# Retention by 64 tokens of two batches at a time, with every small matmul on a quarter of the array

## The chip, the cores and the metric

The kernel runs on one core of a Trainium2 chip. Its time is the device time of one execution in microseconds (us). All operands are fp32. The profile calls TensorE's matmuls PE and its weight loads PEld; DVE is VectorE, ACT is ScalarE, POOL is GpSimd, and SP is the engine that issues most of the DMAs. TensorE's array has 128 rows (the contracted index) and 128 columns (the partitions of the result). A matmul that contracts over 64 and gives 64 partitions covers a quarter of it, one with 128 and 64 covers half. In the records one fp32 matmul is two MATMUL records, each with a weight load.

## The reference

A retention layer gives 3072 tokens of 512 features, and a two-layer network with the activation h * sigmoid(1.702 h) follows.

```python
# q, k, v: (batch 4, heads 8, tokens 768, dim 64), fp32
gamma = 1 - 2 ** (-5 - arange(8))
state = 0
for t in range(768):
    state = gamma * state + outer(k[:, :, t], v[:, :, t])     # 64 x 64 per batch and head
    y[:, :, t] = q[:, :, t] @ state / sqrt(64)
x = y as (3072 tokens, 512)
h = x @ w_in                                                  # 512 x 2048
out = (h / (1 + exp(-1.702 * h))) @ w_out                     # 2048 x 512
```

The weights come in as 64-bit numbers.

## The kernel before

**Blocks.** The 3072 tokens are worked on in six blocks of 512. Retention makes x of a block, `up0`, `up1` (blocks 0 and 1) or `up` (the others) multiply it by w_in, `hidden` applies the activation, and `down` multiplies by w_out. `up` and `down` use a scheme of seven products in place of eight (the `sums_*` functions form the operands), on full 128x128 weights.

**Chunks.** Retention goes by 24 chunks of 128 tokens of one batch, so a sequence has six chunks (`NC`). With c the place in the sequence, a chunk has these steps for its eight heads:

- `turn`: q and k are brought to (dim, token). For chunks 0 to 7 ("early") by TensorE transposes with the identity and two ACT copies (line 242); for the others ("late") by DVE transposes (line 245) of tiles that 32 small DMAs per chunk put in the right blocks (line 148).
- `scores` (line 269): k times q, contraction over the 64 dims, for 128 keys by 128 queries, in two halves of the keys: quarter-array matmuls with 128 moving columns. Late chunks leave out the queries ahead of the keys' half, so half of their scores matmuls have 64 columns.
- `decayed`: DVE multiplies the scores by the decay mask (line 295 early, lines 288, 291 and 292 late), giving `at`. Late chunks keep `at` in a layout of their own (`at2`, `moved`), with a second set of decay columns (`cold2`) and a rebuilt mask.
- `finish`: q times the old state (line 328, quarter array, not for c = 0); `at` times v added to it in the same PSUM (line 328, mostly half array: 128 keys contracted, 64 columns); k decayed (`kd`, a POOL multiply at line 260) times v (line 351, half array, not for the last c), for the state. DVE then scales the sum into X (line 355) and updates the state (line 358 or 361, after a POOL multiply at line 360).

`attend(j, f)` issues the scores of chunk j and the finish of chunk f.

**Weights.** `fetch` starts a 512 KB DMA of raw weights on SP's queue (line 175) into one of three buffers. `narrow` turns 64-bit weights into fp32 with one ACT step (line 204) and six DVE steps (lines 205 to 214), and fetches again. There are 2 narrow calls of half size and 15 of full size.

**Order.** TensorE runs in the order in which the program gives its instructions; for the other engines a planner chooses the order within the dependencies, except for instructions marked `keep_in_program_order`. The program issues chunk 0 to 4 with narrows and the first three `up0` units; then 13 `up0` units with chunks 5 to 7 between them; then 16 `up1` units; then `down(0)`, `down(1)`, and for blocks 2 to 5 `up` and `down`. The late chunks sit between units of `down`. At the start SP gets the loads of chunk 0 (q and v; k goes on ACT's queue), one weight fetch, the loads of chunk 1, and one more fetch. POOL's queue loads `cold` and `rowd`; the mask is built from `cold` by eight DVE copies (line 548) and one POOL select (line 551). `keep_warm` issues TensorE transposes whose results are not used.

Of the kernel before, what the change touches and what calls it, by code (L numbers as in the profile page):

```python
# [9 lines left out]
F32 = mybir.dt.float32  # L10
# [18 lines left out]
def kernel(  # L29
# [36 lines left out]
    NC = S // P  # L66
    NCH = B * NC
# [8 lines left out]
    assert 2 * D == P and HP * P == DM and S % P == 0 and NCH % CB == 0 and DM == 512 and NFF == 16  # L76
# [19 lines left out]
    rowd = const.tile([P, HP, P], F32, name="rowd")  # L96
    cold = const.tile([P, 2 * H], F32, name="cold")
    cold2 = const.tile([P, 2 * H], F32, name="cold2")
    at2 = const.tile([P, 2, HP, P], F32, name="at2")
    whole = const.tile([P, 2, 2], F32, name="whole")  # L100
    ident = const.tile([P, P], F32, name="ident")
    mask = const.tile([P, 2, HP, P], F32, name="mask")
    state = [const.tile([P, HP, D], F32, name=f"state{i}") for i in range(2)]
# [4 lines left out]
    def late(j):  # L108

        return j >= 2 * CB

    def moved(r, s):

        return r ^ s // 2

    def load(j, what="qkv"):


        b, c = divmod(j, NC)
        rows = slice(c * P, (c + 1) * P)

        def plain(name, src, tag, bufs, pairs=False, engine=sp):
            t = two.tile([P, H, D], F32, name=name + "_in", tag=tag, bufs=bufs)
            QKV[name, j] = t
            src = src[b, :, rows, :].rearrange("h p d -> p h d")
            if late(j):
                for i in range(2):
                    sp.dma_start(t[:, 6 * i:6 * i + 2, :], src[:, 6 * i:6 * i + 2, :])  # L130
                    sp.dma_start(t[i * D:(i + 1) * D, 2:6, :], src[(1 - i) * D:(2 - i) * D, 2:6, :])
            elif pairs:
                for i in range(2):
                    engine.dma_start(t[:, i:H:2, :], src[:, i * HP:(i + 1) * HP, :])
            else:
                sp.dma_start(t, src)

        if j < 2 * CB:
            if "q" in what:
                plain("q", q, "q_sq", 2, True)  # L140
                plain("kn", k, "k_sq", 2, True, sp if j else act)
        elif "q" in what:
            for name, src in (("q", q), ("k", k)):
                t = two.tile([P, HP, P // C4, C4], F32, name=name + "_sq")
                for r0 in range(0, P, C4):
                    d0 = r0 % D
                    for hp in range(HP):
                        tc.keep_in_program_order(sp.dma_start(
                            t[r0:r0 + C4, hp],
                            src[b, hp + HP * (r0 // D), rows, d0:d0 + C4].rearrange("(s p) d -> p s d", p=C4)))  # L150
                QKV[name, j] = t
        if "v" in what:
            if j >= 2 * CB and c < NC - 1:
                plain("kn", k, "kn", 1)
            plain("v", v, "v", 2)
# [62 lines left out]

    QT, KT, KD, AT = {}, {}, {}, {}

    def home(j, name):

        at = ["qT", "kT", "kd", "at"].index(name)
        shape = [[HP, P], [HP, P], [H, D], [2, HP, P]][at]
        if j >= 2 * CB:
            return at2 if at == 3 else one.tile([P] + shape, F32, name=name, tag=name, bufs=2 - (at > 0))
        if at < 3:
            t = G[:, at, j % 2 * 2:j % 2 * 2 + 2]
            return t.rearrange("p s t -> p (s t)").rearrange("p (a b) -> p a b", a=shape[0])
        return G[:, 3 + j % 2].rearrange("p s t -> p (s t)").rearrange("p (a b c) -> p a b c", a=2, b=HP)  # L230

    def turn(j, between=lambda: None):

        early = j < 2 * CB
        for name, store in (("q", QT), ("k", KT)):
            t = home(j, name + "T")
            if early:
                x = QKV["kn", j] if name == "k" else QKV.pop(("q", j))
                p = ps.tile([P, HP, P], F32, name="pt", tag="y")
                for hp in range(HP):  # L240
                    pe.transpose(p[:, hp, :], x[:, 2 * hp:2 * hp + 2, :].rearrange("p i d -> p (i d)"), ident)
                act.activation(t, p, AF.Copy)
                between()
            else:
                tc.keep_in_program_order(dve.transpose(
                    t.rearrange("p h t -> p (h t)"), QKV.pop((name, j)).rearrange("p h s d -> p (h s d)")))
            store[j] = t
        if early:
            decay(j)
        if j + 2 < NCH and (j + 2 < 2 * CB or not early):  # L250
            load(j + 2, "qk")

    def decay(j):

        if j % NC == NC - 1:
            return
        KD[j] = home(j, "kd")
        x = QKV.pop(("kn", j)).rearrange("p h d -> p (h d)")
        x = x.rearrange("p (s r d) -> p r s d", s=HP, r=2) if j < 2 * CB else x.rearrange("p (r s d) -> p r s d", r=2, s=HP)
        pool.tensor_mul(KD[j].rearrange("p (r s) d -> p r s d", r=2), x,  # L260
                        (cold2 if late(j) else cold)[:, H:2 * H].rearrange("p (r s) -> p r s", r=2)[:, :, :, None].to_broadcast([P, 2, HP, D]))

    def scores(j):
        p = ps_a.tile([P, 2, HP, P], F32, name="pa", tag="pa")
        kt, qt = KT.pop(j), QT[j]

        def product(r, s, h, t0):
            c, k = (h ^ moved(r, s) if late(j) else h) * D, slice(r * D, (r + 1) * D)
            pe.matmul(p[c:c + D, r, s, t0:], kt[k, s, h * D:(h + 1) * D], qt[k, s, t0:], start=True, stop=True)  # L269

        if late(j):

            for s in range(2):
                for r, o, h in ((0, 0, 0), (0, 0, 1), (1, 0, 1), (1, 0, 0), (0, 2, 0), (1, 2, 0), (0, 2, 1), (1, 2, 1)):
                    product(r, s + o, h, h * D)
        else:
            for s in range(HP):
                for h in range(2):
                    for r in range(2):
                        product(r, s, h, 0)  # L280
        return p

    def decayed(j, p):

        a = AT[j] = home(j, "at")
        if late(j):

            dve.tensor_mul(a[:, :, :, D:], p[:, :, :, D:], mask[:, :, :, D:])  # L288
            a, x, m = [t.rearrange("p r s t -> p (r s) t") for t in (a, p, mask)]
            a2, x2, m2 = [t[:D].rearrange("p (g e) t -> p g e t", g=4)[:, 0:4:3, :, :D] for t in (a, x, m)]  # L290
            dve.tensor_mul(a2, x2, m2)
            dve.tensor_mul(a[D:, 2:6, :D], x[D:, 2:6, :D], m[D:, 2:6, :D])
        else:
            for i in range(2):
                dve.tensor_mul(a[:, i], p[:, i], mask[:, i])  # L295

    def attend(j, f=None):


        p = []  # L300
        if f is not None:
            finish(f, lambda: j is not None and p.append(scores(j)))
        else:
            p.append(scores(j))
        if j is not None:
            decayed(j, p[0])
            if j > 2 * CB:
                decay(j)
        if f is not None and f + 2 < 2 * CB:
            load(f + 2, "v")  # L310
        if j is not None and 2 * CB < j < NCH - 1:
            load(j + 1, "v")

    def finish(j, between):
        c = j % NC
        old, new = state[c % 2], state[(c + 1) % 2]
        vn, a, qt = QKV.pop(("v", j)), AT.pop(j), QT.pop(j)


        y = ps_a.tile([P, 2, HP, P], F32, name="py", tag="py")  # L320
        heads = [(s, r) for s in range(HP) for r in range(2)]
        started = set()

        def add(r, s, v, x, t):

            first = (r, s % 2) not in started
            started.add((r, s % 2))
            pe.matmul(y[s % 2 * D:(s % 2 + 1) * D, r, s // 2, t], v, x, start=first, stop=False, skip_group_check=True)  # L328

        if not late(j):  # L330
            between()
        if c:
            for s, r in heads:
                k = slice(r * D, (r + 1) * D)
                add(r, s, old[k, s, :], qt[k, s, :], slice(0, P))
        if late(j):


            for s, r in heads[:HP]:
                k = slice(r * D, (r + 1) * D)  # L340
                add(r, s, vn[k, HP * r + s, :], a[k, r, s, :D], slice(0, D))
            between()
        for s, r in heads:
            t = slice(D if late(j) and s < 2 else 0, P)
            add(r, s, vn[:, HP * r + s, :], a[:, r, s, t], t)
        if c < NC - 1:

            kd = KD.pop(j)
            u = y[:, 0, 2:4, :].rearrange("p o t -> p (o t)").rearrange("p (s d) -> p s d", s=HP)
            for s, r in heads:  # L350
                pe.matmul(u[r * D:(r + 1) * D, s, :], kd[:, HP * r + s, :], vn[:, HP * r + s, :],  # L351
                          start=False, stop=True, skip_group_check=True)
        half, t0 = divmod(j % CB * P, TH)
        x = X1 if j // CB == 1 else X
# [325 lines left out]
```

## Time and profile before

| what | value |
|---|---|
| median of 16 runs | 699.07 us (698.22 to 700.41) |
| the profiled execution's own time | 699.25 us |
| its span in the profile | 697.5 us |
| PE, DVE, ACT, POOL busy | 98%, 52%, 18%, 20% of the span |
| bytes moved by DMA | 46.4 MB |

The span runs from the first to the last instruction of the profiled execution. A group of instructions is named by engine, line, and out<-in tiles; "mean" is the duration of one record, and as matmuls overlap, durations do not add up to time. The windows view gives busy time of each engine in a stretch, with the number of records in brackets. The chain of waits is followed back from the last instruction; its pieces are start, length and what ran.

### The profile page before, as it was taken

The numbers are of one execution on the slowest core, as the hardware profiler recorded it, in microseconds if no ns is written. First come the engines' busy times: TensorE is split into PE (matmuls) and PEld (weight loads), VectorE is DVE, ScalarE is ACT, GpSimd is POOL, SyncE is SP. The second block draws the span as 40 slices with busy tenths as digits, with TensorE's granted clock in tenths as the row PEclk, the third lists the DMA queues.
The fourth block names the chain that finished last, engine by engine and source line by source line (L and its number), as shares of the span: only waits on it lengthen the run. The fifth ranks groups of instructions, "written<-read, shape, count | busy, mean of one in ns | idle before, by whom it ended". The sixth has DMA issues, their size and how long they took to land.

```text
span 697.5 us, 11471 instructions
## 1 busy us (share of the span) xinstructions
PE 680.9 (98%) x4621; PEld 569.1 (82%) x4621; DVE 365.1 (52%) x541; ACT 125.8 (18%) x197; POOL 137.6 (20%) x137
## 2 busy tenths in 40 slices
PE   6699999999999999999999999999999999999997
PEld 5588885446888888888888888888888888888886
DVE  2998889994710843443652444463345372344241
ACT  2213333221000001332000332000333000233000
POOL 4211031000366414000324100134100143000030
PEclk9999999999999999999999999999999999999999
DMA  9995443522121223200323320323320210000001
GB/s 212 264 221 166 136 137 111 157 35 32 29 35 57 62 43 94 50 13 14 69 42 73 70 41 8 66 35 73 70 42 2 51 40 17 30 1 1 15 1 45
DMA packets 140404, 46.40 MB, mean 67 GB/s; under 512 B 131824, under 2 KB 132864, under 8 KB 140352
## 3 DMA queue, kind: packets, MB, share of 16 engines
q1 hardware_dynamic: 136096, 38.84, 24.8%
q0 software_dynamic: 2112, 5.53, 2.3%
q10 hardware_dynamic: 2144, 1.31, 0.6%
q8 instruction: 36, 0.59, 0.4%
q14 instruction: 16, 0.13, 0.1%
HBM read 39.34 MB, written 6.29 MB: 65 GB/s over the span
## 4 chain that ended last, share of the span: by engine, by line
PE 88%; DVE 7%; DMA 2%; SPq 1%; ACT 1%; issue 1%; POOL 1%; ACTq 0%; DVEq 0%; POOLq 0%
PE pd L491 39%; PE px L440 16%; PE py L440 12%; PE ph L401 8%; PE py L328 5%; PE ph L388 5%; PE pa L269 2%; PE py L351 1%; DMA kn_in<-in_k_dram 1%; DMA W<-in_moe_w_in_dram 1%; DVE W L430 1%; DVE G L430 1%; DVE W L214 1%; DVE W L210 1%; DVE G L295 1%
## 5 line engine op out<-in xcount | busy, mean ns | idle before, releaser
L491 PE MATMUL pd<-W,G 128*128 128x256 f32 x1120 | 247.4, 381 | 0.4 <-DVE G L431 0.3
L491 PEld LDWEIGHTS pd<-W,G 128*128 128x128 f32 x1120 | 211.3, 190 | 30.6 <-DVE G L431 1.2
L440 PE MATMUL px<-X,W 128*128 128x256 f32 x512 | 119.0, 379 | 0.0
L440 PEld LDWEIGHTS px<-X,W 128*128 128x128 f32 x512 | 97.3, 190 | 13.2
L440 PE MATMUL py<-X,W 128*128 128x256 f32 x384 | 90.7, 379 | 0.0
L440 PEld LDWEIGHTS py<-X,W 128*128 128x128 f32 x384 | 73.0, 190 | 9.9
L388 PE MATMUL ph<-X,W 128*128 128x256 f32 x256 | 58.0, 383 | 1.6 <-DVE W L214 0.9
L401 PE MATMUL ph<-W,W 128*128 128x512 f32 x128 | 55.2, 593 | 0.2 <-DVE W L355 0.2
L260 POOL TENSOR_TENSOR kd<-kn_in,cold 128x512 f32<-128x512 f32 x13 | 13.7, 1056 | 210.7 <-DMA k_sq<-in_k_dram 117.0
L388 PEld LDWEIGHTS ph<-X,W 128*128 128x128 f32 x256 | 47.8, 190 | 8.8 <-DVE W L214 1.3
L288 DVE TENSOR_TENSOR at<-pa,mask 128x512 f32<-128x512 f32 x16 | 11.0, 689 | 74.1 <-PE py L328 65.4
L401 PEld LDWEIGHTS ph<-W,W 128*128 128x128 f32 x128 | 24.2, 190 | 30.7 <-issue 28.5
L432 POOL TENSOR_TENSOR G<-G 128x512 f32<-128x512 f32 x20 | 29.5, 1481 | 95.0 <-DVE G L431 93.6
L369 DVE TENSOR_TENSOR G<-G,sg 128x512 f32<-128x512 f32 x48 | 33.0, 689 | 13.7 <-ACT sg L367 13.7
L367 ACT ACTIVATE sg<-G 128x512 f32<-128x512 f32 x48 | 30.2, 630 | 51.0 <-DVE G L450 30.7
L483 POOL DMA_DIRECT2D out_dram<-o x20 | 14.9, 748 | 119.9 <-DVE o L482 119.9
L367 ACT ACTIVATE sg<-ph 128x512 f32<-128x512 f32 x32 | 19.2, 600 | 100.1 <-PE ph L388 48.9
L491 PE MATMUL pd<-W,W 128*128 128x256 f32 x160 | 35.8, 381 | 0.4 <-DVE W L431 0.3
L491 PEld LDWEIGHTS pd<-W,W 128*128 128x128 f32 x160 | 30.2, 190 | 5.6 <-DVE W L431 1.2
L450 DVE TENSOR_TENSOR G<-py,p 128x512 f32<-128x512 f32 x16 | 11.1, 692 | 37.7 <-PE py L440 37.7
L478 ACT ACTIVATE u<-pd 128x512 f32<-128x512 f32 x6 | 3.6, 597 | 146.0 <-PE pd L491 146.0
L482 DVE TENSOR_TENSOR o<-pd,vv 128x512 f32<-128x512 f32 x12 | 7.7, 686 | 34.9 <-ACT vv L478 34.9
(106 smaller groups left out, 679.1 us busy)
## 6 DMA issues: line engine op xcount, KB each, us to landing
W<-in_moe_w_in_dram SPq DMA_DIRECT2D x12, 512.0 KB, 4.9
W<-in_moe_w_out_dram SPq DMA_DIRECT2D x10, 512.0 KB, 4.2
out_dram<-o POOLq DMA_DIRECT2D x20, 256.0 KB, 2.8
v_in<-in_v_dram SPq DMA_DIRECT2D x64, 64.0 KB, 2.4
q_sq<-in_q_dram SPq DMA_DIRECT2D x256, 16.0 KB, 1.8
k_sq<-in_k_dram SPq DMA_DIRECT2D x256, 16.0 KB, 1.8
kn_in<-in_k_dram SPq DMA_DIRECT2D x52, 64.0 KB, 2.4
G<-in_moe_w_out_dram SPq DMA_DIRECT2D x6, 512.0 KB, 3.9
```

What stands on the lines that cost most here:

```text
L260: pool.tensor_mul(KD[j].rearrange("p (r s) d -> p r s d", r=2), x, (cold2 if late(j) else cold)[:, H:2 * H].rearrange("p (r s) -> p r s", ...
L269: pe.matmul(p[c:c + D, r, s, t0:], kt[k, s, h * D:(h + 1) * D], qt[k, s, t0:], start=True, stop=True)
L328: pe.matmul(y[s % 2 * D:(s % 2 + 1) * D, r, s // 2, t], v, x, start=first, stop=False, skip_group_check=True)
L367: act.activation(s, h, AF.Sigmoid, scale=1.702)
L369: dve.tensor_mul(g, h[:, i], s[:, i])
L388: pe.matmul(h[:, ab], w, X[:, 2 * half + c // 2, c % 2, :], start=(ab == 0 and c == 0), stop=(c == 3), skip_group_check=True)
L401: pe.matmul(h, w, X1[:, c // 2:4:2, c % 2, :], start=(c == 0), stop=(c == 3))
L430: dve.tensor_sub(a[2], a[0], a[2])
L432: pool.tensor_sub(a[1], a[1], a[0])
L440: pe.matmul(acc[:, u, :], W1[:, 2 * d + u, sa, c, :], X[:, sb, c, :], start=(start and u == 0 and c == 0), stop=(stop and c == 1), skip_gr ...
L483: (pool if m < NB - 1 else act).dma_start(rows[th, e], o)
L491: pe.matmul(p0[:, n, :], g1(m, p, sa)[:, n * P:(n + 1) * P], W2[:, sb, p, :], start=(new and p == 0 and n == 0), stop=(last and p == NP - ...
```

## The change

A chunk is now 64 tokens of two batches: partitions 0 to 63 hold one batch, 64 to 127 the other. There are still 24 chunks, in two sequences of twelve (`NC = S // D`), and four of them still make a block of 512 tokens. Every small matmul has a contraction of 64, 64 columns and 64 moving columns, and is issued so that four in a row lie on the four quarters: the scores, k times v, q times the state, `at` times v, and the early turns, which are matmuls with the identity now and no transposes. q times the state is no longer added to `at` times v in PSUM: it has a region of its own, and DVE multiplies it by `rowd` and adds the rest. The update of the state lies in the second half of the `pa` tile and no longer in `py`. The special layouts of late chunks (`at2`, `moved`, `cold2`, the second mask) are gone.

At the start the first weight fetch goes ahead of v of chunk 0 and the second ahead of the loads of chunk 1, a narrow is called ahead of `turn(0)`, `rowd` and the mask come from one DMA, and the order of the first chunks changes.

```diff
-    NC = S // P
-    NCH = B * NC
+    NC = S // D
+    NCH = B // 2 * NC
...
-    state = [const.tile([P, HP, D], F32, name=f"state{i}") for i in range(2)]
+    state = [const.tile([P, 2, HP, D], F32, name=f"state{i}") for i in range(2)]
...
+            for i in range(2):
+                engine.dma_start(t[i * D:(i + 1) * D], src[b + i, :, rows, :].rearrange("h p d -> p h d"))
...
-                    for hp in range(HP):
+                    for n in range(P // C4):
+                        t0 = c * D + n * C4 % D
                         tc.keep_in_program_order(sp.dma_start(
-                            t[r0:r0 + C4, hp],
-                            src[b, hp + HP * (r0 // D), rows, d0:d0 + C4].rearrange("(s p) d -> p s d", p=C4)))
+                            t[r0:r0 + C4, :, n], src[b + n * C4 // D, h0:h0 + HP, t0:t0 + C4, d0:d0 + C4]
+                            .rearrange("h p d -> p h d")))
...
+    HALF = [slice(i * D, (i + 1) * D) for i in range(2)]
+    TWO = [(i, r) for i in range(2) for r in range(2)]
...
+            x = QKV.pop(("q", j)), QKV["kn", j]
+            p = [ps.tile([P, 2, HP, D], F32, name="pt", tag="y") for i in range(2)]
+            order = [(n, s, i, r) for n in range(2) for s in range(HP) for i, r in TWO]
+            for n, s, i, r in sorted(order, key=lambda o: o[2]) if j == 0 else order:
+                pe.matmul(p[i][HALF[r], n, s, :], x[n][HALF[i], HP * r + s, :], ident[HALF[i], HALF[i]],
+                          start=True, stop=True)
...
+            for i in range(2):
+                act.activation(t[:, :, :, HALF[i]], p[i], AF.Copy)
...
+    def attend(j, f=None):
+
+        pa = ps_a.tile([P, 2, 2, HP, D], F32, name="pa", tag="pa")
+        if j is not None:
             for s in range(HP):
+                for r, i in TWO:
+                    pe.matmul(pa[HALF[i], r, 0, s, :], KT[j][HALF[r], s, HALF[i]], QT[j][HALF[r], s, HALF[i]],
+                              start=True, stop=True)
+            KT.pop(j)
+        if f is not None:
+            c = f % NC
+            old, new = state[c % 2], state[(c + 1) % 2]
+            vn, a, qt = QKV.pop(("v", f)), AT.pop(f), QT.pop(f)
+            if c < NC - 1:
+                kd = KD.pop(f)
+                for s in range(HP):
+                    for i, r in TWO:
+                        pe.matmul(pa[HALF[r], i, 1, s, :], kd[HALF[i], HP * r + s, :], vn[HALF[i], HP * r + s, :],
+                                  start=True, stop=True)
+            py = ps_a.tile([P, 2, 2, 2, P], F32, name="py", tag="py")
+            if c:
+                for s2 in range(2):
+                    for i in range(2):
+                        for r, o in TWO:
+                            pe.matmul(py[HALF[o], r, 1, i, s2 * D:(s2 + 1) * D], old[HALF[r], i, 2 * s2 + o, :],
+                                      qt[HALF[r], 2 * s2 + o, HALF[i]], start=True, stop=True)
+            for s2 in range(2):
+                for r in range(2):
+                    for i, o in TWO:
+                        s = 2 * s2 + o
+                        pe.matmul(py[HALF[o], i, 0, r, s2 * D:(s2 + 1) * D], vn[HALF[i], HP * r + s, :],
+                                  a[HALF[i], r, s, :], start=True, stop=True)
+        if j is not None:
+            AT[j] = home(j, "at")
+            dve.tensor_mul(AT[j], pa[:, :, 0], mask)
             if j > 2 * CB:
                 decay(j)
+        if f is not None:
...
+            if c:
+                tmp = two.tile([P, 2, 2, P], F32, name="tmp", bufs=1)
+                dve.tensor_mul(tmp, py[:, :, 1].rearrange("p r i t -> p i r t"),
+                               rowd.rearrange("p (r s) t -> p r (s t)", r=2)[:, None].to_broadcast([P, 2, 2, P]))
+                dve.tensor_add(x, y, tmp.rearrange(by, t=D))
+            else:
+                act.activation(x, y, AF.Copy)
+            u = pa[:, :, 1]
+            if c == 0:
+                dve.tensor_copy(new, u)
+            elif c < NC - 1:
+                pool.tensor_mul(new, old, whole[:, None, :, None].to_broadcast([P, 2, HP, D]))
+                dve.tensor_add(new, new, u)
+            if f + 2 < 2 * CB:
+                load(f + 2, "v")
...
-    load(0)
+    load(0, "qk")
     make_identity(nc, ident)
...
+        pool.dma_start(cold[HALF[i]].rearrange("p (n h) -> p n h", n=2),
+                       bass.AP(tensor=col_decay.tensor, offset=col_decay.offset, ap=[[W, D], [D * W + H, 2], [1, H]]))
+    pool.dma_start(m3, bass.AP(tensor=row_decay.tensor, offset=row_decay.offset, ap=[[0, P], [P, H], [1, D]]))
...
     fetch()
+    load(0, "v")
+    fetch()
     load(1)
-    fetch()
...
+    for o in range(2):
+        act.activation(rowd[HALF[o]], m3[HALF[o], o:H:2, :], AF.Copy)
+
+    dve.tensor_mul(m3, m3, cold[:, 0:H, None].to_broadcast([P, H, D]))
+    for i in range(2):
+        pool.affine_select(out=m3[HALF[i]], in_=m3[HALF[i]], compare_op=ALU.is_ge, fill=0.0, base=0,
+                           pattern=[[0, H], [1, D]], channel_multiplier=-1)
...
     keep_warm(7)
-    turn(0, lambda: keep_warm(3))
+    narrow()
+    turn(0)
...
+    attend(0)
+    narrow()
     for _ in range(2):
         fetch()
+    turn(1)
+    attend(1, 0)
+    for _ in range(2):
+        fetch()
+    turn(2)
+    for j in range(2, 5):
+        attend(j, j - 1)
+        turn(j + 1)
         narrow()
+        up0(0, j - 2, "x")
+    between = [lambda j=j: (attend(j, j - 1), turn(j + 1)) for j in (5, 6)] + [lambda: attend(7, 6), lambda: attend(None, 7)]
...
-        if n in (0, 2, 4, 6, 8, 9, 11):
+        if n in (1, 4, 7, 10):
             between.pop(0)()
-
-    tc.keep_in_program_order(pool.memset(at2, 0.0))
...
-                tc.keep_in_program_order(pool.dma_start(cold2[to, c], col_decay[src, c]))
-    make_mask(range(2, 6), cold2, [(slice(0, D), D), (slice(D, P), 0)])
```

## The prediction

> **What bounds the kernel now.** I read the page's busy shares and its slices first, then the chain of waits, then windows, and timelines where a chunk of retention runs.
>
> ```profile
> span 697.5 us, 11471 instructions
> ...
> PE 680.9 (98%) x4621; PEld 569.1 (82%) x4621; DVE 365.1 (52%) x541; ACT 125.8 (18%) x197; POOL 137.6 (20%) x137
> ...
> PE   6699999999999999999999999999999999999997
> ...
> DVE  2998889994710843443652444463345372344241
> ```
>
> TensorE is busy nearly all the time, but DVE is too in slices 2 to 9 (17 to 157 us). Windows give the size of that:
>
> ```profile
> core 0: us, PE busy (x) PEld busy (x) DVE busy (x) ACT busy (x) POOL busy (x), PEclk, DMA share, GB/s
> 10.00:163.50 153.50, 145.02 (x1000) 101.17 (x1001) 137.79 (x191) 43.19 (x62) 22.06 (x26) 0.98 0.58 153
> 0.00:42.30 42.30, 31.20 (x341) 25.57 (x341) 28.67 (x49) 12.32 (x18) 15.45 (x22) 0.92 1.03 237
> 42.30:697.50 655.20, 649.72 (x4280) 543.50 (x4280) 336.44 (x493) 113.46 (x180) 122.14 (x115) 1.00 0.23 56
> 33.20:36.60 3.40, 3.03 (x31) 2.91 (x32) 3.00 (x5) 0.00 (x0) 0.12 (x1) 0.50 0.77 224
> ```
>
> Up to 42.3 us TensorE is idle 11.1 us and the DMA engines are full (share 1.03); after that only the last waits on output leave it idle. From 10 to 163.5 DVE has 15.7 us to spare. So there are three stages: a start bound by DMA and DVE, a stretch to 163.5 where TensorE leads and DVE follows closely, and the rest, bound by TensorE alone. What a late chunk costs is in the chain and in TensorE's timeline:
>
> ```profile
> 321.86 10.36 PE pd L491 x48
> ...
> 334.50 10.56 PE pd L491 x48
> 345.06 0.71 PE py L328 x24
> 345.77 0.67 PE pa L269 x22
> 346.44 0.87 PE py L328 x16
> 347.31 0.47 PE py L351 x16
> 347.77 2.35 PE pd L491 x10
> ```
>
> ```profile
> 345.47 0.29 PE L328 MATMUL py<-at,v_in 64*64 64x64 f32 x8
> 345.59 0.85 PE L269 MATMUL pa<-qT,kT 64*64 64x128 f32 x32
> ```
>
> From one burst of 48 `pd` records to the next is 13.27 us (334.50 to 347.77), and a burst with no chunk ahead of it takes 10.36: a full chunk costs 2.91 us of a saturated engine.
>
> **The change: late chunks.** 10.36 / 48 is 0.216 us per record of 256 columns, 0.843 ns a column. A full chunk has, in columns divided by the quarters that run together: scores (16 x 128 + 16 x 64) / 4 = 768, state 16 x 128 / 4 = 512, `at` times v 8 x 64 / 4 + (8 x 64 + 8 x 128) / 2 = 896, kd times v 16 x 64 / 2 = 512; 2688 in all, 2.27 us. The other 0.64 us is pace (pairs of half-array records of 64 columns take 0.46 / 8 = 57.5 ns, not 54) and the changes into the chunk, from quarters to halves and out. After, a full chunk is 128 records, 32 groups of four: at 57.5 ns a group 1.84 us. No change from quarters to halves is left; I keep 0.30 for going in and out: 2.14. The pieces for chunks without state or kd are 24 groups, 1.68; for the lone scores 0.75 and the lone finish 1.25. After: 13 x 2.14 + 2 x 1.68 + 2.0 = 33.2. Before: 11 full ones, four of about 2.45 (2.28 between bursts at 332.22, and edges), 1.0 and 1.75: 44.6. **Gain 11.4 us**, all of it on the path.
>
> [...] The x32 row shows 32 starts within 0.85 less the last one's 0.22, so 20 ns apart, and the x8 row 8 starts within 0.07. [...]
>
> **Early chunks.** `up1` starts at 108.5, and the first `up0` unit ends at 27.6. Between lie 15 units of 16 x 0.216 = 3.45, 51.8, and 29.1 for retention and gaps. After, the work behind that first unit is attends of 32, 32, 32, 32, 32 and 24 groups and four turns of 64 records, 16 groups: 248 groups, 14.3, and six runs with 0.3 each: 16.1. **13.0 less.**
>
> Against it, that first unit comes later: it now stands behind attend(2, 1) and turn(3), so it needs k of chunk 3.
>
> ```profile
> 24.82 1.04 POOL L260 TENSOR_TENSOR G<-kn_in,cold 128x512 f32<-128x512 f32 x1 [4.55 <-DMA kn_in<-in_k_dram]
> ```
>
> So that k has landed by 24.8 now, behind about 5.3 MB. SP's order after puts one more 0.5 MB weight fetch ahead of it (both early fetches, the narrow's ahead of q and k of chunk 2, then three), at the 0.285 MB/us of 10 to 30 us: 1.8 later, 26.6. Turn(3) 1.0 and the unit 3.5 make 31.1. TensorE then has had gaps of several us. [...] I add 0.9: unit ends at 32.0, **4.4 later**.
>
> DVE. Per early chunk before: 2 x 0.68 + 0.69 + 0.41 = 2.46; after: mask 0.69, scaling 0.69, sum 0.69, state of twice the size 0.69 = 2.76. Seven chunks add 2.1; chunk 0's x goes to ACT, -0.7; the mask's copies (12 x 0.22, of which two waits) go, one multiply of 0.69 comes: about level. In the rounds of chunks 2 to 4 DVE has 5.8 (a narrow) + 2.76 + 0.69 = 9.3 to do per 6.4 of TensorE. The narrows started 1 to 4 us sooner hide most of it; the next thing late is the third weight pair's narrow, or scores that wait for `pa`, which now is free only when the state is added. **1.6 lost**. Up to 157 DVE then has 15.7 - 7 = 9 us to spare.
>
> **At nothing.** Late DVE 2.62 to 2.76 per chunk: it is busy 45% there; without that cover 16 x 0.14 = 2.2. POOL: state multiply 0.73 to about 1.1, next needed 10 us on; start: three DMA issues either way; two half selects for one; the later memset, eight `cold` issues (4.94) and selects go. The mask is later by about 5 us (DMA of 256 KB landing near 10, two ACT copies, a multiply, selects: 13 for 8.1), but `at` of chunk 0 is now wanted after turn(1), near 16. ACT's first narrow may stand ahead of turn(0)'s copies: up to 3, covered by the same wait for q and k of chunk 1. SP: v and kn four issues of 0.6 to two, q and k 32 as before. The two `keep_warm` of 3 go. Early turns cost 16 groups, 0.92, for 0.87.
>
> **Sum.** 697.5 - 11.4 - (13.0 - 4.4 - 1.6 = 7.0) = 679.1 of span; the execution's own time is 1.75 over its span: 680.9, and that execution is 0.18 over the median. Predicted 681.
>
> **Rivals.**
> [...]
> (2) *The start eats the early gain.* First unit ending at 39 instead of 32 through mask, q and k behind weights, or `up0` waiting for narrows of a full DVE: 688. For: DMA share 1.03, DVE 9.2 and 9.6 of 10 in 20 to 40. Against: a narrow is ready sooner, and `up0` has 8 to 10 us of lead from its fourth weight pair on.
> (3) *The start goes better*, fewer gaps and a warm clock: 671 to 675.
> (4) *The change doesn't do what it says*: the planner orders DVE or ACT so that the quarters wait, or matmuls of two row halves hold each other up; TensorE gains nothing late: 692 with the early gain, 699 without.
>
> **How the numbers follow.** Likeliest, 68%: 675 to 687, at 681. (2) 11%: 687 to 692. (1) in full 9%, 705 to 715; in part 4%, about half of that below the old time. (3) 5%. (4) 3%. A change of 0.2% (1.4 us) is about what a measurement of this kernel can tell from none. Faster: 68 + 11 + 5 + 2 or so, less a little for what I overlook, 0.84; same 0.03; slower 0.13. The range 673 to 695 takes in the first two, part of (3) and (4): over 8 in 10.
>
> **What would show it.** Right: late full chunks 2.1 us between bursts in the chain; line 269's successor, kd, state and `at` rows all 64x64 with 64 columns and groups 57 ns apart; `up1` starting near 101 and `down(0)` near 156; DVE over 93% from 10 to 156. Wrong: chunks of 2.8 us or more (rival 1), `up1` later than 106 (rival 2), TensorE waits on DVE's mask multiply or state add after 45 us.

## The result, and the profile after

The changed kernel takes 692.49 us (median of 9 runs, 689.69 to 693.28) beside 699.22 (48 runs) for the kernel before: a ratio of 0.9898 [0.9889, 0.9907]. It is faster by 6.7 us where 18 were forecast. The direction, and the gain of the late chunks, came as written; the gain of the early part did not come at all. (The time alone would also fit rival 4, which had 692 with the gains the other way round; the stages below tell the two apart.)

The page of the changed kernel, in the rows shown of before: its span, busy times, the slices of TensorE and DVE, and the row of the queue that fetches instructions (number of fetches, MB, share):

```profile
span 690.9 us, 14320 instructions
...
PE 669.8 (97%) x6087; PEld 561.2 (81%) x6087; DVE 369.6 (53%) x512; ACT 127.7 (18%) x201; POOL 144.4 (21%) x131
...
PE   5879999999999999999999999999999999999997
...
DVE  3598999997431563444463345373345373344241
...
q8 instruction: 48, 0.79, 0.5%
```

TensorE has 1466 matmul records more and 11.1 us less of busy time, but its span falls by 6.6 only: it is busy 97% of the span instead of 98, and the slices under 9 are now the first three instead of two.

The chain of waits of the changed kernel (start us, length us, engine, group), around a late full chunk and at the two marks between the stages, and behind it the same two marks in the kernel before:

```profile
112.11 55.20 PE ph L347 x128
167.31 10.36 PE pd L439 x48
...
229.78 10.56 PE pd L439 x48
242.36 10.56 PE pd L439 x48
```

```profile
108.51 55.20 PE ph L401 x128
163.71 10.36 PE pd L491 x48
```

From burst to burst is 242.36 - 229.78 = 12.58 us; less the bare 10.36, a full chunk costs 2.22 (before: 2.91). The marks divide the result. `up1` starts at 112.11 where it started at 108.51, and `down(0)` at 167.31 where it started at 163.71: the kernel is **3.6 us behind the old one** there. From `down(0)` to the end of the span it takes 690.9 - 167.31 = 523.6 instead of 697.5 - 163.71 = 533.8: **10.2 us are won**. Together 6.6.

TensorE's timeline in that chunk (start us, time from first start to last end, engine, line, output and inputs, tile, shapes, count):

```profile
240.26 0.69 PE L252 MATMUL pa<-qT,kT 64*64 64x64 f32 x32
240.78 0.65 PE L263 MATMUL pa<-v_in,kd 64*64 64x64 f32 x32
241.25 0.65 PE L272 MATMUL py<-qT,state 64*64 64x64 f32 x32
241.71 0.65 PE L278 MATMUL py<-at,v_in 64*64 64x64 f32 x32
```

The sections begin 0.46 to 0.52 us apart: 14.5 ns for each of 32 starts on average, 16 in the first section. No slowing is seen over the 128 records.

**Where the early part goes.** Windows of the kernel before, and then, in the same columns, of the changed kernel (stretch and its length, busy time and count of each engine, granted clock, DMA share, GB/s):

```profile
core 0: us, PE busy (x) PEld busy (x) DVE busy (x) ACT busy (x) POOL busy (x), PEclk, DMA share, GB/s
10.00:20.00 10.00, 7.46 (x98) 6.07 (x98) 6.40 (x12) 3.58 (x6) 4.96 (x6) 0.83 1.20 285
20.00:30.00 10.00, 7.91 (x98) 6.39 (x102) 9.17 (x15) 3.46 (x5) 2.33 (x3) 1.00 1.11 293
```

```profile
10.00:20.00 10.00, 6.85 (x209) 6.29 (x213) 8.77 (x13) 3.86 (x8) 5.29 (x6) 1.00 0.95 228
20.00:30.00 10.00, 6.92 (x249) 6.45 (x241) 5.17 (x8) 1.57 (x3) 3.93 (x4) 0.72 0.81 229
...
48.30:55.10 6.80, 5.68 (x14) 4.56 (x15) 5.91 (x7) 0.00 (x0) 1.04 (x1) 0.50 0.77 225
```

Three things are read here. From 10 to 30 us the transfers move 228 to 229 GB/s instead of 285 to 293, and their engines are no longer full (share 0.81 to 0.95). DVE, which was busy 9.2 of 10 us at 20 to 30, is busy 5.2: the engine that held the start back before now waits itself. And the clock is at half in a stretch of 6.8 us in the middle of dense products.

The 1.00 of the changed kernel at 10 to 20 us is not a reading. Its trace has no clock record before 20.9 us (that of the kernel before none before 9.3), and the view counts time without a record as full clock. The pace says otherwise: 32 of the small records, 0.65 us in the late chunk above, take 1.16 here, and they take 1.16 again at 19.54.

```profile
18.69 1.16 PE L278 MATMUL py<-G,v_in 64*64 64x64 f32 x32
```

So the changed kernel does its small matmuls at about half pace up to 20.9 us; what that costs was not separated.

What TensorE waits for in this kernel (us in total, times, longest):

```profile
PE ph L334 <- DVE W L196: 4.6, 2, 3.4
PE pa L252 <- ACT G L229: 4.4, 2, 3.9
...
PE pt L224 <- DMA q_in<-in_q_dram: 1.4, 2, 1.2
```

The first row, waits for weights, is followed up here. Of the second, 3.9 us lie ahead of the first scores, up to 12.3 us; q of chunk 1, which TensorE needs next, lands only at 12.8, so little of it can be lost. The timeline shows what DVE waits for (in brackets the idle time before, and what ended it):

```profile
27.83 1.40 PE L224 MATMUL pt<-ident,q_in 64*64 64x64 f32 x30 [1.19 <-DMA q_in<-in_q_dram]
...
30.10 1.09 ACT L229 ACTIVATE G<-pt 128x512 f32<-128x512 f32 x2 [7.64 <-PE pt L224]
30.12 4.21 PE L334 MATMUL ph<-X,W 128*128 128x256 f32 x16
31.08 1.14 ACT L186 ACTIVATE W<-W 128x1024 f32<-128x1024 f32 x1
32.24 0.69 DVE L187 TENSOR_SCALAR W<-W 128x1024 f32<-128x1024 f32 x1 [4.15 <-ACT W L186]
...
39.34 3.72 PE L334 MATMUL ph<-X,W 128*128 128x256 f32 x16 [1.23 <-DVE W L196]
...
49.42 13.38 PE L334 MATMUL ph<-X,W 128*128 128x256 f32 x48 [3.38 <-DVE W L196]
```

q of chunk 3 is there at 27.8; turn(3) runs, and ACT, which has stood 7.64 us before turn(3)'s copies (L229), makes them at 30.10. Only then comes the first step of the third narrow, on ACT at 31.08 (L186), for in the program it stands behind the turn. DVE has stood 4.15 us for it. So this narrow's last step starts at 38.07 (the kernel before: 31.70), that of the fourth at 48.15 (39.57), and the second and third units of `up0` wait 1.23 and 3.38 us for weights. The third unit starts at 49.42 instead of 46.04, and from it to `up1` are 62.7 us instead of 62.5.

### The profile page after: what moved, and what is told of

It reads as the page before. It is cut to its first block, busy times and chain, and to the rows that moved or that the text cites. A ratio compares the mean times of both kernels' runs of the same rounds, so it can differ in the third digit from the quotient of the medians.

```text
span 690.9 us, 14320 instructions
## 1 busy us (share of the span) xinstructions
PE 669.8 (97%) x6087; PEld 561.2 (81%) x6087; DVE 369.6 (53%) x512; ACT 127.7 (18%) x201; POOL 144.4 (21%) x131
## 3 DMA queue, kind: packets, MB, share of 16 engines
q1 hardware_dynamic: 136352, 39.10, 24.5%
## 4 chain that ended last, share of the span: by engine, by line
PE 87%; DVE 9%; DMA 2%; ACT 1%; issue 0%; POOL 0%; POOLq 0%; ACTq 0%
PE pd L439 40%; PE px L386 16%; PE py L386 12%; PE ph L347 8%; PE ph L334 5%; PE pa L252 2%; PE py L278 1%; PE pa L263 1%; DMA q_in<-in_q_dram 1%; PE py L272 1%; DMA mask<-in_row_decay_dram 1%; PE pt L224 1%; DVE W L196 1%; DVE W L376 1%; DVE G L376 1%; DVE W L315 1%
## 5 line engine op out<-in xcount | busy, mean ns | idle before, releaser
L334 PE MATMUL ph<-X,W 128*128 128x256 f32 x256 | 60.4, 397 | 5.3 <-DVE W L196 4.6
L334 PEld LDWEIGHTS ph<-X,W 128*128 128x128 f32 x256 | 50.4, 199 | 13.2 <-DVE W L196 4.9
L244 POOL TENSOR_TENSOR kd<-kn_in,cold 128x512 f32<-128x512 f32 x14 | 16.3, 1168 | 190.6 <-PE pa L263 161.5
L282 DVE TENSOR_TENSOR at<-pa,mask 128x512 f32<-128x512 f32 x16 | 11.0, 686 | 62.1 <-PE pa L263 53.7
L302 POOL TENSOR_TENSOR state<-state,whole 128x512 f32<-128x512 f32 x20 | 22.0, 1098 | 64.5 <-DVE state L303 59.0
L396 DVE TENSOR_TENSOR G<-py,p 128x512 f32<-128x512 f32 x16 | 11.1, 692 | 37.7 <-PE py L386 37.7
```

What stands on the lines that cost most here:

```text
L244: keep(pool.tensor_mul(KD[j], QKV.pop(("kn", j)), cold[:, H:2 * H, None].to_broadcast([P, H, D])))
L302: pool.tensor_mul(new, old, whole[:, None, :, None].to_broadcast([P, 2, HP, D]))
L334: pe.matmul(h[:, ab], w, X[:, 2 * half + c // 2, c % 2, :], start=(ab == 0 and c == 0), stop=(c == 3), skip_group_check=True)
```

## Experiments

All lines are those of the changed kernel, and `...` or a remark in brackets marks what is left out. Ratios are to the kernel before on the same chip, beside the changed kernel's 0.9898. Each profile is one execution.

**1. Narrow ahead of attend and turn**, with the two fetches left where they were (`narrow(False)` narrows and leaves its two fetches to the lines below):

```
     for j in range(2, 5):
+        narrow(False)
         attend(j, j - 1)
         turn(j + 1)
-        narrow()
+        for _ in range(2):
+            fetch()
         up0(0, j - 2, "x")
```

> The changed kernel with the narrows of the rounds of chunks 2 to 4 called ahead of the round's attend and turn instead of behind them (their two fetches stay where they were, so SP's order is the same). Theory A (the early gain was lost because ACT's first step of the third narrow stands behind the copies of turn(3), which wait for q of chunk 3, so DVE idles from 28 to 32 us and the second and third weight pairs come late): that ACT step runs near 23 us, not 31; TensorE's waits on line 196 (4.6 us) fall below 1.5, the half clock from 48 to 55 us goes, up1 starts near 105 to 107 instead of 112.1, and the time is 684 to 688. Theory B (DVE has too much work up to the end of the up0 units, whatever its order): the narrows end earlier but other DVE work comes later; up1 stays within 1.5 us of 112 and the time within 1.5 of the changed kernel's. Theory C (the loads are late): as B, with waits on DMA in place of those on DVE.

Measured 693.76 us, 0.992 [0.9902, 0.9939]: no gain. The third narrow's ACT step is at 23.23 instead of 31.08 and its last step at 31.76 instead of 38.07, as wanted, and no wait on weights is left in TensorE's waits. But the time comes back in other places. In the waits of TensorE of this kernel (us in total, times, longest) and, behind that, its timeline:

```profile
PE ph L334 <- issue: 3.2, 1, 3.2
...
PE ph L334 <- DVE X L295: 1.9, 2, 1.3
PE pt L224 <- issue: 1.3, 1, 1.3
```

```profile
31.89 6.24 PE L334 MATMUL ph<-X,W 128*128 128x256 f32 x16 [1.26 <-DVE X L295]
38.66 1.21 ACT L186 ACTIVATE W<-G 128x1024 f32<-128x1024 f32 x1
...
44.90 6.12 PE L334 MATMUL ph<-X,W 128*128 128x256 f32 x14 [3.17 <-issue]
```

The X addition now stands among the narrow's DVE steps, so the first unit starts at 31.89 and not at 30.12; it runs below full clock (0.70 on average from 31.2 to 48.3 us; 6.24 for 16 records where 3.72 is usual); the fourth narrow's ACT step is held up behind that unit's sigmoid; and the second unit loses 3.17 us to "issue", a wait that no semaphore of an engine or of a transfer of data ends (the last section comes back to it). `up1` starts at 115.0. Moving the narrow early enough is thus not by itself the cure.

**2. The unit of `up0` ahead of the turn**, narrow behind as it was:

```
     for j in range(2, 5):
         attend(j, j - 1)
+        up0(0, j - 2, "x")
         turn(j + 1)
         narrow()
-        up0(0, j - 2, "x")
```

> The changed kernel with the up0 unit of the rounds of chunks 2 to 4 ahead of turn(j+1) in TensorE's order, the narrow still behind the turn. Theory C (the start is late because the first up0 unit stands behind q of chunk 3): the first unit starts near 28 us instead of 30.1 and covers the wait for q; 1 to 3 us gained. Theory A: the first unit starts sooner, but the second one waits for its weights as before: gain under 1.5 us, and the wait on line 196 grows by what was gained. Theory B: no gain at up1.

Measured 709.25 us, 1.0137 [1.0123, 1.0152]: 17 us slower than the changed kernel. TensorE's waits of this kernel, and its narrows on ACT in the timeline:

```profile
PE ph L334 <- DVE W L196: 15.1, 2, 7.8
```

```profile
34.97 1.16 ACT L186 ACTIVATE W<-W 128x1024 f32<-128x1024 f32 x1
52.30 1.17 ACT L186 ACTIVATE W<-G 128x1024 f32<-128x1024 f32 x1
```

The first unit is sooner by a microsecond (29.1), but now each narrow's first step stands on ACT behind the turn's copies and the sigmoid of the unit ahead. Its weights come 4 to 13 us later (31.08 becomes 34.97, 39.10 becomes 52.30), and 15.1 us of waiting for weights, 10.5 more than in the changed kernel, are most of the loss; other waits grow with them. This is the mechanism of the changed kernel in a stronger dose: who stands ahead of L186 on ACT sets when `up0` has weights.

**3. Load order of before**: chunk 0's v with its q and k, ahead of the first weights, and chunk 1 one fetch sooner.

```
-    load(0, "qk")
+    load(0)
 ...
     fetch()
-    load(0, "v")
-    fetch()
     load(1)
+    fetch()
```

> The changed kernel with SP's first loads in the order of the kernel before: q and v of chunk 0, first weight fetch, chunk 1, second weight fetch. Theory C (weights ahead of the chunks' loads delay the retention chain): q of chunk 1 and scores of chunk 1 come about 2 us sooner, q of chunk 3 is not sooner as the bytes ahead of it are the same: within 1 us of the changed kernel. Theory A: the second narrow comes about 3 us later, and with it the first up0 unit or the third narrow: 0 to 3 us slower.

Measured 695.61 us, 0.9945 [0.9932, 0.9958]: 3 us slower than the changed kernel, with `up1` at 114.0. The changed kernel's load order, weights ahead of v and chunk 1 behind the second fetch, is thus a gain of about that size (the intervals are apart), so this part of the change is not what ate the early gain.

**4. Experiments 1 and 2 together**: narrow first, then attend, unit, turn.

```
     for j in range(2, 5):
+        narrow(False)
         attend(j, j - 1)
+        up0(0, j - 2, "x")
         turn(j + 1)
-        narrow()
-        up0(0, j - 2, "x")
+        for _ in range(2):
+            fetch()
```

> The changed kernel with both edits: narrow ahead of the round, and the up0 unit ahead of turn(j+1). Theory A with C: the gains add: up1 near 103 to 105, time 682 to 686. Theory B: up1 is held by DVE near 109 to 112 and both edits together give no more than the better one, under 2 us.

Measured 695.67 us, 0.9944 [0.9927, 0.9962]; `up1` at 114.3. With the narrow ahead of it the early unit no longer costs 17 us, only 3: the loss of experiment 2 was the narrow's place, not the unit's.

**5. Fillers for the clock**: 30, 10, 10, 10 and 28 unused transposes put into the gaps of the start (the tile that they write is made anew at each call).

```
+    keep_warm(30)
     attend(0)
...
     for j in range(2, 5):
+        if j == 2:
+            keep_warm(10)
         attend(j, j - 1)
+        if j == 2:
+            keep_warm(10)
         turn(j + 1)
         narrow()
+        if j > 2:
+            keep_warm(10 if j == 3 else 28)
         up0(0, j - 2, "x")
```

> The changed kernel with unused TensorE transposes (keep_warm) put in front of the places where TensorE waits in the start: 30 ahead of attend(0), 10 each ahead of attend(2, 1), turn(3) and the second up0 unit, 28 ahead of the third. Theory D (half the loss after the third unit is the clock: 48 to 55 us at 0.50 costs 2.8 us, 24 to 31 us another 1 to 2): the granted clock stays near full from 20 to 55 us, up1 starts 2.5 to 4 us sooner, 688.5 to 690. Theory A (the narrows come late because their first step stands behind TensorE's results on ACT): the waits for the weights stay, fillers take their place, and what the clock gives back before them is lost in them: gain only the 2.8 us after the third unit, or less. If a filler is longer than the wait, it costs up to 3 us.

Measured 699.33 us, 1.0002 [0.9989, 1.0016]: 7 us worse. The clock at half shrinks to three stretches of 3.41 us (mean granted clock of the span 0.993, in the changed kernel 0.989), and full clock is on record from 12.7 us instead of 20.9, but TensorE's waits of this kernel say where the time goes:

```profile
PE pt L224 <- issue: 5.0, 4, 1.9
...
PE py L278 <- issue: 1.0, 1, 1.0
```

Six microseconds of "issue" in all, and the fillers themselves, which stand in TensorE's queue for 13.6 us, take more than the clock gave back. The half clock is therefore not shown to be the whole cause by this run, nor excluded.

**6. Two narrows early, one in the next round**: the third and fourth narrow ahead of attend(2, 1), the fifth ahead of attend(3, 2), fetches in place.

```
     for j in range(2, 5):
+        for _ in range([2, 1, 0][j - 2]):
+            narrow(False)
         attend(j, j - 1)
         turn(j + 1)
-        narrow()
+        for _ in range(2):
+            fetch()
         up0(0, j - 2, "x")
```

> The changed kernel with the third and the fourth narrow called ahead of attend(2, 1) and the fifth ahead of attend(3, 2) (fetches where they were), so that on ACT no sigmoid and no copy of a later turn stands ahead of them. Theory A: the second and third weight pairs are ready near 32 and 40 us, not 39.3 and 49.4; the third unit no longer waits for its weights; up1 3 to 5 us sooner, 687 to 690. Theory D: the first unit is not sooner and runs at half clock as in the first experiment; under 1.5 us of gain.

Measured 690.84 us, 0.9881 [0.9863, 0.9899]. That is below the changed kernel's 0.9898, but the intervals overlap; the profile has `up1` 1.8 us sooner (110.29). Its waits of TensorE and a window:

```profile
PE pa L252 <- ACT G L229: 3.8, 2, 3.2
PE pt L224 <- DMA q_in<-in_q_dram: 3.4, 1, 3.4
...
PE ph L334 <- issue: 1.1, 1, 1.1
```

```profile
27.30:37.50 10.20, 7.77 (x77) 6.47 (x78) 10.06 (x12) 2.23 (x3) 3.34 (x2) 0.50 0.75 194
```

No wait for weights (it was 4.6) and DVE full, 10.06 of 10.2 us; but q of chunk 3 is still not there before 28.3, and the clock is at half for 10.2 us. Of the 4.6 us of waits 1.8 came through.

**7. A cheaper narrow.** For w_in's chunks three DVE steps instead of six; left out are the low word and the right exponent of each number:

```
+        if i >= NFF:
             (the four steps L189 to L192, as before)
+        else:
+            dve.tensor_scalar(hi, hi, 0x807FFFFF, 0x3F000000, op0=ALU.bitwise_and, op1=ALU.bitwise_or)
+            lo = hi
```

> The changed kernel with the narrows of w_in cut down from six DVE steps to three (the numbers of w_in are not the right ones): the weights of the up0 units cost DVE 2.6 us a pair and no longer 5.8. Theory A and B (the early gain was lost in DVE's chain of narrows): waits on weights go, up1 starts near 100 to 103 us, and the time is 679 to 684. Theory C and D (loads or the clock): up1 stays within 3 us of 112, time 689 to 692.

**8. The same cut in the kernel before.**

> The kernel before with the same cut of w_in's narrows. Theory A: it was bound by TensorE in the up0 units already, so it gains only its own waits of the start, 1 to 4 us: 695 to 698, and against it the changed kernel with the cut is 13 to 18 us faster, as much as the prediction had for the change. Theory B': it gains as much as the changed kernel does (8 to 12 us), so the cut shows nothing about the change.

Measured: the changed kernel with the cut 688.36 us, 0.9856 [0.9823, 0.9889]; the kernel before with the cut 699.14, 0.9995 [0.9983, 1.0006]. The changed kernel gains about 2.9 us by it (0.9898 - 0.9856, of 699.4; the intervals touch at 0.9889, so the gain is hardly clear of noise), the old one nothing. DVE's work on weights, or when it is done, thus seems to hold the changed start a little and did not hold the old one; but even with half of it gone most of the 10.6 us that the start lacks beside the forecast stays missing. TensorE's waits of the cut kernel, in an execution with a span of 692.4 us, the longest of its runs and longer than the changed kernel's 690.9, so that it shows what came in place of the waits and not where 2.9 us were won (its lines are 4 higher: L228 is the turn, L256 the scores, L282 `at` times v, L338 the unit):

```profile
PE pt L228 <- DMA q_in<-in_q_dram: 4.5, 3, 2.2
PE pa L256 <- ACT G L233: 4.2, 2, 3.5
...
PE py L282 <- issue: 2.4, 1, 2.4
PE ph L338 <- issue: 1.5, 1, 1.5
```

No wait on weights is left, and in its place stand q's transfers, 4.5 us, and "issue", 3.9 in these two rows and 0.6 in a third.

## Why the prediction was right for the late chunks and wrong for the start

**Late chunks: right.** Forecast 2.14 us a chunk and a gain of 11.4; measured 2.22 and 10.2. The work was sized from the rows (57.5 ns for a group of four; the trace has 4 x 14.5 = 58). The time of 705 to 715 that rival 1 has in the chances rests on an interval between starts that no run shows; what the trace of the changed kernel shows is 128 starts in a row, 14.5 to 16 ns apart on average. That it is the four quarters running together which allows this was not tried by itself; the rows show the pace, not its cause.

**Early part: wrong, by 10.6 us.** The sum had -7.0: 13.0 less work behind the first unit, 4.4 for a later first unit, 1.6 for DVE. `up1` came 3.6 later instead.

- *The first unit 4.4 later* is the smaller error: it ends at 34.25, 6.65 after the 27.6 of before. q of chunk 3 is there at 27.8 and not, with k, at 26.6, for the step took the old 0.285 MB/us for a start that moves 0.228; and the clock is at half (0.50 from 24.3 to 31.1 us) under the turn and the unit's beginning. The 0.9 that the forecast adds for this unit is shown by no run; in its place the turn took 2.29 us (27.83 to 30.12) and the unit 4.13 (to 34.25), where 1.0 and 3.5 were written.
- *13.0 less work, 1.6 lost on DVE* is the step that failed. Behind the first unit, 15 units and retention took 80.9 us before and 77.9 after (112.11 - 34.25): 3.0 won where 13.0 - 1.6 = 11.4 were written. The windows of these stretches, of the kernel before and then of the changed one, show why:

```profile
27.60:46.09 18.49, 14.82 (x226) 12.57 (x225) 17.95 (x23) 5.52 (x8) 2.58 (x2) 0.91 0.97 233
46.09:108.51 62.42, 62.24 (x505) 53.78 (x505) 53.11 (x75) 17.11 (x26) 9.91 (x13) 1.00 0.50 142
```

```profile
34.25:49.42 15.17, 10.35 (x402) 9.13 (x401) 14.97 (x18) 5.45 (x8) 4.00 (x3) 0.96 0.74 185
49.42:112.11 62.69, 61.74 (x832) 53.36 (x832) 58.43 (x80) 16.52 (x24) 8.94 (x7) 0.96 0.52 153
```

  The prediction set the old 29.1 us, gaps included, against a new 16.1 with no gaps. Of the old 29.1, idle TensorE was 3.8 and its stretch at half clock (3.03 busy of 3.40 us at 33.2 to 36.6) cost about 1.5 (half of 3.03): 23.8 of work. The new stretch, less its 51.8 of units, is 26.1: idle 4.8 and 0.95, half clock at 48.3 to 55.1 about 2.8 (half of 5.68), and 17.5 of work, near the 16.1. So the work fell by 6.3 and not by 13.0, and idle time and half clock, which were to vanish, grew by 3.2; all that the prediction had against them was the 1.6 for DVE.
- *Why the gaps.* The prediction counted DVE's busy time in these rounds (9.3 to do per 6.4) and took it that "narrows started 1 to 4 us sooner hide most of it". The trace shows the third narrow's first step only at 31.08, with DVE idle for 4.15 ahead of it. What was missed is a place in a queue: this step is on ACT, in order behind copies that need turn(3), so q of chunk 3. The amount of work then keeps the delay from being made up: from 34.25 to 49.42 DVE is busy 14.97 of 15.17 us. Experiment 2 deepens that place and loses 17 us, experiment 4 takes the loss back, and experiment 6 removes the wait on weights.
- *Why removing them gives so little.* Experiments 1, 6 and 7 each leave no wait on weights, and gain by their ratios -1.5, 1.2 and 2.9 us, the first two inside their intervals. Each time another end comes up: q of the chunk (1.4 us of waits becomes 3.4 in 6 and 4.5 in 7), half clock, "issue". The likely reading is that the start has several chains that end within a few microseconds of each other. That one queue place made the waits on weights is shown; what sets the time of the start as a whole is not, for no run here won back more than 2.9 of the 10.6 us.

This is rival 2, "the start eats the early gain" (688 forecast, first unit at 39 or weights late), which had 11%. It went further than rival 2 was priced at, by 4.5 us, and its first form did not come: the first unit ended at 34.25 and not at 39. Weights ahead of v, the other suspect, is a gain of 3 (experiment 3).

Why the transfers of 10 to 30 us average 228 GB/s is in part in the trace. The new shape, one transfer for a batch over 64 partitions, is not slower where the engines have work: at 24 to 25 us, with q and k of chunk 3, they move 284 GB/s, and the kernel before with packets of the same 256 bytes moves 220 at 30 to 31. But there are holes. A load of v stands in SP's queue for 2.8 us until TensorE has read the buffer, SP's next issue, a weight fetch, is at 27.93 us, and meanwhile the transfers run dry:

```profile
SPq L117 <- PE py L278: 3.2, 2, 2.8
```

```profile
26.00:28.00 2.00, 0.81 (x26) 0.66 (x19) 1.54 (x3) 0.00 (x0) 1.04 (x1) 0.50 0.08 17
```

A share of 0.08 of 16 engines is little more than one engine. By the trace's packets, 1899 of the 2048 of q and k of chunk 3 had gone by 25.8 us; the rest follow one behind the other, and turn(3) waits for them until 27.8. Why this last part is 2 us behind was not tried; a 16 KB fetch of instructions runs from 25.71 to 26.82.

Still open: the share of the half clock, which was not separated from that of the gaps ahead of it, and what the start would be with all of these ends removed at once.

## What to carry to other kernels

Less work on TensorE was a gain where it was saturated, in the late chunks: there the sum of rows by columns held to 1.2 us in 11.4. In a start with gaps, a forecast must follow each queue in order: for a step on ACT or DVE, ask which instruction stands ahead of it and whose data that needs, and count gaps and clock anew instead of letting them go with the work. And where several waits end close together, try the removal of one before counting on it: here three such cures gave between -1.5 and 2.9 us.

## What the runs showed of the hardware

- **Pace of quarter matmuls.** The records of 64x64 fp32 matmuls of 64 columns, dealt over four quarters, start every 14.5 ns on average within a section of 32 (16 in the first section), and 128 follow each other so (240.26 to 242.29 us).
- **"Issue" waits of TensorE.** With 2849 instructions more, the program makes 48 instruction fetches instead of 36 (0.79 MB for 0.59). Up to 130 us TensorE waits for nothing but "issue" 0.9 us in the changed kernel, 1.3 in experiment 3, 1.8 in 6, 4.5 in 1, 4.4 in 7, 6.0 in 5, and not at all in experiments 2 and 4 or in the two runs with the old order. The number of fetches alone does not make these waits, for experiments 2 and 4 have the same 48. But each of the 15 waits over 0.25 us ends 1.25 to 1.55 us after a 16 KB packet of the instruction queue has ended (in the changed kernel the packets end at 17.01 and 22.44 and the waits at 18.42 and 23.79; in experiment 1 the packet ends at 43.45 and the wait of 3.17 at 44.90). That TensorE waited there for its next instructions is the author's reading of these times; no run was made to change the fetches alone.
- **Half clock behind stretches in which TensorE was partly busy.** The clock records of the traces last 3.41 us or a multiple of it (6.83, 17.07), apart from the last of each trace. In the changed kernel half clock begins at 24.3 and at 48.2 us, and in the 3.4 us ahead of either TensorE was busy for 1.50 and 1.23 us:

```profile
20.90:24.30 3.40, 1.50 (x79) 1.26 (x75) 1.63 (x3) 1.09 (x2) 1.68 (x2) 1.00 1.05 358
44.80:48.20 3.40, 1.23 (x84) 1.09 (x76) 3.37 (x6) 2.09 (x3) 1.02 (x1) 1.00 0.67 148
```

  Each time it lasts 6.8 us; in the second case 5.68 of them are busy with dense products, which by the author's estimate (half of 5.68) costs about 2.8 us. TensorE was busy for 44% and 36% of the stretches ahead of the two; what brings the half clock on was not tried.
